# Routed experts: a plain fp32 quarter of the second product, casts on ScalarE alone, one written order

## The chip, the core and the metric

The kernel runs on one core of a Trainium2 chip. The metric is the device time of one execution in microseconds (us). A core has a matrix engine (TensorE, PE in the rows; PEld is its weight load), a vector engine (VectorE, DVE), an activation engine (ScalarE, ACT), GpSimd (POOL), SyncE (SP), which here issues nearly all transfers, and 16 DMA engines. Each engine runs its own instructions in the order in which the program holds them, and waits on semaphores for the others.

## What is computed

The reference chains three parts on 1536 rows (2 batches of 768) of 512 columns, all in fp32. The first is attention with 8 heads, a local window of 96 keys, 8 global keys and a distance bias. The second sends each row with a positive skip score to one of 8 experts; the third runs all 4 experts of a second set on every row and adds them, weighted:

```python
h = np.maximum(xc[mask] @ w1[e], 0.0)            # routed, e of 8: w1 512x1024, w2 1024x512
y[mask] = gate_w[mask, None] * (h @ w2[e])
...
h = np.maximum(x @ w1[e], 0.0)                   # second set, e of 4
out += p[:, e:e + 1] * (h @ w2[e])
```

## The kernel before

**Stages.** Set-up and attention fill the first 131 us of the profiled span: 24 units of half a tile (12 tiles of 128 rows, two groups of heads). Then come the routed experts, to about 262 us, and the second set in 48 steps to the end. This text is mainly on the routed experts.

**One product in three.** Fp32 products are made of `fp32r` matmuls. An operand is split into a high part, a cast to `fp32r`, and a low part, the raw value minus the high part. `mm3` (L108 to L111) then issues three matmuls into the same PSUM bank: high by high (L109), high by low (L110), low by high (L111). A raw weight tile w{i}x is 128x1024 fp32, 512 KB; `split_w` (L91) casts it into one of 12 high tiles (wx0x to wx3x, wh0x to wh7x, used in turn; L97 where ScalarE casts, L101 where GpSimd does), and VectorE subtracts (L68). The low part r{i}x takes the place of w{i}x, one of 20 places.

**One routed expert.** An expert's 128 rows of input are transposed and split into xq (`x_parts`). `layer1` is the first product: 4 weight tiles, 2 banks, 3 matmuls each, so 24 matmuls of 512 columns. `hidden` (L571) takes the ReLU into hs; `h_parts` transposes hs in two halves of four 128x128 blocks and splits them into shh and shl, from the PSUM tile pt; `layer2` (L583 to L587) is the second product: 4 weight tiles, f = 0 to 7, again 24 matmuls, into psy; `rows_of` copies psy to yt (L677) and sends it to memory. The table `SCH_M1` (L106) gives for tile s = 0 to 3 of a product who casts and who subtracts: ScalarE casts s = 0 and 2, GpSimd s = 1 and 3, VectorE does all subtractions.

**What sets the order.** Under `tc.manual_schedule()` an engine's instructions stand as the code calls them. Before, three stretches are under it (the attention loop, the routed experts, the second set), and the set-up ahead of the attention loop is ordered by the scheduler. The loop of the routed experts overlaps neighbours: while PE makes the first product of expert e and then the second of e-1, the other engines split the first weights of e+1, take `hidden` of e, transpose the input of e+1, and split the second weights of e. On ScalarE, for instance, the casts for e+1's first product stand ahead of `hidden` of e. SP fetches weights into the 20 places as the low parts in them have been read for the last time.

**After the routed experts.** The last expert's product is mixed with work for the second set: four tiles of output rows are gathered by GpSimd, sums of the second set's first weights, and their splits.

Of the kernel before, what the change touches and what calls it, by code (L numbers as in the profile page):

```python
# [8 lines left out]
F32 = mybir.dt.float32  # L9
# [35 lines left out]
def attention_moe_moe(ctx: ExitStack, tc: tile.TileContext, qkv, nints_d, wg, w1, w2, dprob, u1, u2, out):  # L45
# [57 lines left out]
                sub_lo(nc.vector if le == "V" else nc.gpsimd, lo[:, a], raw[:, a], hi[:, a])  # L103
        return hi, lo

    SCH_M1 = [[("A", "V")], [("G", "V")], [("A", "V")], [("G", "V")]]  # L106

    def mm3(o, ah, al, bh, bl, start, stop):  # L108
        nc.tensor.matmul(o, ah, bh, start=start, stop=False)  # L109
# [1 line left out]
        nc.tensor.matmul(o, al, bh, start=False, stop=stop)  # L111


    wxx = ExitStack()
    wxp = wxx.enter_context(tc.tile_pool(name="wxp", bufs=1))
    wx = [wxp.tile([P, 1024], F32R, name=f"wx{n}x") for n in range(4)]
# [156 lines left out]
    def load_qk(t):  # L273
        nc.sync.dma_start(qkr[t % 2], qkv[t, :, 0:2])
# [40 lines left out]
    with ExitStack() as c2:  # L315
# [41 lines left out]
        def prep_q(t):  # L357
            qs[t] = qh, ql = xq[t % 2]
            raw = qkr[t % 2][:, 0].rearrange("p (d t) -> p d t", d=NPAIR)
            nc.scalar.activation(out=qh, in_=raw, func=AF.Copy)  # L360
            sub_lo(nc.gpsimd, ql, raw, qh)

        def prep_k(t):
            so = t % 3
            raw = qkr[t % 2][:, 1].rearrange("p (d t) -> p d t", d=NPAIR)
            if t < 2:
                nc.scalar.activation(out=kh[:, so], in_=raw, func=AF.Copy)
            else:
# [12 lines left out]
        def load_gv(t):
            nc.sync.dma_start(gv, qkv[t, 0:GMAX, 2].rearrange("p (h e) -> p h e", h=H))
# [11 lines left out]
        def stage_qk(u):  # L394
            t, g = divmod(u, 2)
            sl, col, ss = slots_of(t)
            nk = len(sl) * P
            qh, ql = qs[t]
            sps[u] = [sbs[(2 * u + n) % 3] for n in range(2)]
            for pp in range(2):  # L400
                pr = 2 * g + pp
                for n, (a, bm) in enumerate(((qh, kh), (qh, kl), (ql, kh))):
                    for h2 in range(2):
                        rows = slice(h2 * HD, (h2 + 1) * HD)
                        nc.tensor.matmul(sps[u][h2][:, pp, 0:nk], a[rows, pr, :], bm[rows, ss, pr, :], start=(n == 0), stop=(n == 2))
# [63 lines left out]
        def run(fs):  # L469
            for f in fs:  # L470
                f()

        NU = 2 * NT
        with tc.manual_schedule():
            load_v(0)
            nc.gpsimd.memset(vv[:, :, :, HD:HV], 1.0)
            prep_q(0)
            prep_k(0)
            save_gk(0)
            load_qk(2)  # L480
            make_bias(slice(512, 640))
            for u in range(-2, NU + 5):
                t, g = divmod(u, 2)
                if u < 2:
                    warm(WARMS[u + 2])
                if u + 2 < NU:
                    stage_qk(u + 2)
                if 0 <= u - 2 < NU:
                    run(norm(u - 2))
                if g == 0:  # L490
                    if 0 <= t - 2 < NT:
                        run(rts[t - 2]["steps"][0])
                    if t + 1 < NT and t >= 0:
                        load_v(t + 1)
                    if t in (0, NI):
                        load_gv(t)
                    if t + 2 < NT and t >= 0:
                        prep_k(t + 2)
                        save_gk(t + 2)
                        prep_q(t + 2)  # L500
                    if t + 4 < NT and t >= 0:
                        load_qk(t + 4)
                    if 0 <= t - 3 < NT:
                        put_row(t - 3)
                else:
                    if 0 <= t - 2 < NT:
                        run(rts[t - 2]["steps"][1])
                    if 0 <= t - 1 < NT and 0 < (t - 1) % NI < NI - 1:
                        over_v(t - 1)
                    if 0 < (t + 1) % NI < NI - 1 and t + 1 < NT:  # L510
                        over_k(t + 1)
                    if 0 <= t < NT:
                        stage_d(t)
                if 0 <= u + 1 < NU:
                    stage_e(u + 1)
                if 0 <= u < NU:
                    stage_t(u, 0)
                    stage_t(u, 1)
                if u + 2 < NU:
                    run(stage_s(u + 2))  # L520
                if u == -2:
                    prep_q(1)
                    prep_k(1)
                    load_qk(3)
                if u == -1:
                    make_bias(slice(0, 512))
                if g == 1 and 0 <= t - 1 < NT:
                    stage_x(t - 1)
                if 0 <= u - 1 < NU:
                    stage_pv(u - 1)  # L530
                if g == 1 and 0 <= t - 1 < NT:
                    rts[t - 1]["lg"] = logits(t - 1, xTs[t - 1], ovt[1])
                if g == 0 and 0 <= t - 2 < NT:
                    rts[t - 2]["rk"] = route_rank(t - 2, rts[t - 2]["lg"])
                if 0 <= u < 4:
                    for e in range(2 * u, 2 * u + 2):
                        nc.sync.dma_start(xs[e * P:(e + 1) * P, :], xr[:, NT - 1, :])
                if u == 4:
                    nc.sync.dma_start(ys[0:1, :], xr[0:1, NT - 1, :])
                if g == 0 and 2 <= t < 2 + 2 * ND:  # L540
                    prefetch((t - 2) * 2, (t - 1) * 2)
                if g == 0 and 4 <= t < 4 + 2 * ND:
                    e_, s_ = divmod(t - 4, ND)
                    split_w(wts[t - 4], (wx if e_ else his)[s_], [("A", "V")])
                if u == 6:
                    shares()
                if u == NU - 2:
                    exs.append(qkr[0][:, 0])
                    for t_ in range(NT - NSEL, NT):
                        sels[t_] = a3.tile([P, P], F32, name="sel", tag="sc", bufs=12)  # L550
                if u == NU + 1:
                    pt0, frs = first_rows(ovt[0])
                    frs[0]()
                if u == NU + 2:
                    frs[1]()
            frs[2]()
            split_psum(*xq[0], pt0)
    lpx.close()


# [11 lines left out]
        return hs  # L572

    def h_parts(hs, pool, pst, hp=None, ns=range(2)):
        hh, hl = hp if hp else (pool.tile([P, NF, P], F32R, name=f"sh{m}") for m in "hl")
        pts = {n: transp4(pst, hs[:, n * 512:(n + 1) * 512], tag="pst") for n in ns}
        for n in ns:
            split_psum(hh[:, 4 * n:4 * n + 4, :], hl[:, 4 * n:4 * n + 4, :], pts[n])
        return hh, hl

    def layer2(py, hp, w2s, fs):
        for f in fs:
            w = w2s[f // 2]  # L583
            c = slice((f % 2) * 512, (f % 2) * 512 + 512)
            mm3(py, hp[0][:, f, :], hp[1][:, f, :], w[0][:, c], w[1][:, c], f == 0, f == NF - 1)

    bufs2 = [wts[4:10], wts[10:16]]  # L587

# [14 lines left out]
    with ExitStack() as c2:  # L603
# [3 lines left out]
        psx = c2.enter_context(tc.tile_pool(name="psx", bufs=1, space=PSUM))  # L607
        pst = c2.enter_context(tc.tile_pool(name="pst", bufs=2, space=PSUM))
        psy = c2.enter_context(tc.tile_pool(name="psy", bufs=1, space=PSUM))
        c2.enter_context(tc.manual_schedule())  # L610
        for n in range(2 * ND, NWT):
            raw1[order1[n]] = wts[n]
        nwt[0] = NWT
# [20 lines left out]

        def split1(e, half, part=range(ND)):
            nwh[0] += ND if part[0] == 0 else 0
            return [split_w(raw1[e, half * ND + s], whs[(nwh[0] - ND + s) % 12], SCH_M1[s]) for s in part]

        slf = mp.tile([P, NT], F32, name="slf", bufs=1)
        hps = w2s = None  # L640
# [122 lines left out]
    with ExitStack() as c2:  # L763
        xp = c2.enter_context(tc.tile_pool(name="xp", bufs=1))
        yp = c2.enter_context(tc.tile_pool(name="yp", bufs=3))
        ps = c2.enter_context(tc.tile_pool(name="ps", bufs=1, space=PSUM))
        c2.enter_context(tc.manual_schedule())
        xh = xp.tile([P, 7, 2, T // 2], F32R, name="xh")
        xl = xp.tile([P, 7, 2, T // 2], F32R, name="xl")
        t4 = [xp.tile([P, 2, P], F32, name=f"t4{n}x") for n in range(2)]  # L770
# [179 lines left out]
            pend = (q, c, (hh, hl))  # L950


    ok = nc.values_load(badi[0:1, 0:1], min_val=0, max_val=1)
    with tc.If(ok < 1):
        general(nc, tc, dict(qkv=qkv, ngv=ngv, nlv=nlv, colf=colf, rowf=rowf, xr=xr, ident=ident, transp4=transp4, pas=pas, pr=pr, wgt=wgt,
# [203 lines left out]
```

## Time and profile before

| what | number |
|---|---|
| time, median of 3 runs (772.71, 772.85, 778.5) | 772.85 us |
| the profiled execution: its time, its span | 777.55 us, 775.6 us |
| mean granted TensorE clock over the span, share of full | 0.975 |
| PE busy over the span | 740.3 us (95%) |
| VectorE, ScalarE, GpSimd busy | 550.7 (71%), 294.7 (38%), 294.5 (38%) us |
| chain that ended last, by engine | PE 62%, the others 2% or less each |

The profile is one execution; its span is the time from the first to the last instruction, so 1.95 us of its time lie outside the span. A window row cuts the span and gives for a stretch each engine's busy time and its count of instructions, the granted TensorE clock, the mean busy share of the 16 DMA engines, and what they moved. A waits row says which engine and line waited, for which tile of which engine, for how many us in total, how often, and the longest. A timeline row is one instruction: its start, its duration, engine, line, operation, out<-in, and in brackets how long its engine had been idle before and who ended that. PE's durations overlap, since matmuls are pipelined: what one costs is the distance to the next one's start.

### The profile page before, as it was taken

How to read it: one execution, taken by the hardware profiler on the slowest of the kernel's cores; microseconds unless marked ns; L12 is line 12 of the kernel's file. 1: busy time of each engine (PE TensorE's matmuls, PEld its weight loads, DVE VectorE, ACT ScalarE, POOL GpSimd, SP SyncE). 2: the span in 40 equal slices, each digit the busy share in tenths (PEclk: the TensorE clock that was granted, in tenths of full speed). 3: DMA queues.
4: the chain of work that ended last, by engine and by line, in shares of the span. 5: the costliest groups of instructions: out<-in, count | busy, mean ns of one | idle time of the engine just before them, and what ended most of it. 6: DMA issues, size and time to landing. Idle time of an engine off the chain costs nothing.

```text
span 775.6 us, 12245 instructions
## 1 busy us (share of the span) xinstructions
PE 740.3 (95%) x4810; PEld 665.5 (86%) x4810; DVE 550.7 (71%) x1032; ACT 294.7 (38%) x461; POOL 294.5 (38%) x272
## 2 busy tenths in 40 slices
PE   6999996998889989999999999999999999999996
PEld 6999995876667878999999999999999999999995
DVE  7686875699996979666666666666766666666665
ACT  3876871365353555432232222322322222223111
POOL 5564633244356741474152341441423415314000
PEclk8997998999899999999999999999999999999999
DMA  5866712799663120110010010000100110001003
GB/s 145 283 211 199 239 32 78 282 411 347 238 219 108 55 69 1 53 57 28 28 55 28 28 55 28 28 28 28 55 28 27 49 34 28 28 28 55 1 28 140
DMA packets 36020, 74.90 MB, mean 97 GB/s; under 512 B 15960, under 2 KB 16216, under 8 KB 35954
## 3 DMA queue, kind: packets, MB, share of 16 engines
q1 hardware_dynamic: 34034, 69.39, 26.2%
q0 software_dynamic: 1920, 4.64, 1.9%
q8 instruction: 40, 0.66, 0.3%
q14 instruction: 26, 0.21, 0.1%
HBM read 65.19 MB, written 10.49 MB: 98 GB/s over the span
## 4 chain that ended last, share of the span: by engine, by line
PE 62%; DVE 2%; issue 2%; POOL 2%; DMA 1%; ACT 0%; POOLq 0%; DVEq 0%
PE pf L110 5%; PE pf L109 5%; PE pf L111 5%; PE pg L109 4%; PE pg L110 4%; PE pg L111 4%; PE pa3x L109 3%; PE pa3x L111 3%; PE pa3x L110 3%; PE pa1x L110 3%; PE pa0x L109 3%; PE pa1x L111 3%; PE pa0x L110 3%; PE pa0x L111 3%; PE pa1x L109 3%; PE pa2x L110 3%
## 5 line engine op out<-in xcount | busy, mean ns | idle before, releaser
L908 DVE TENSOR_TENSOR cc<-pg,sf 128x768 f32<-128x768 f32 x48 | 45.9, 957 | 56.8 <-PE pg L111 55.4
L890 ACT ACTIVATE sf<-pf 128x768 f32<-128x768 f32 x48 | 38.9, 811 | 107.3 <-PE pf L111 107.3
L932 ACT ACTIVATE hh0x<-cc 128x1024 fp32r<-128x1024 f32 x24 | 25.5, 1061 | 120.7 <-DVE cc L917 120.7
L932 ACT ACTIVATE hh1x<-cc 128x1024 fp32r<-128x1024 f32 x23 | 24.4, 1060 | 106.4 <-DVE cc L917 106.4
L917 DVE TENSOR_TENSOR cc<-cc,uv 128x768 f32<-128x768 f32 x47 | 52.7, 1121 | 1.6
L933 DVE SCALAR_TENSOR_TENSOR hl0x<-cc,hh0x 128x1024 fp32r<-128x1024 f32 x24 | 29.5, 1231 | 24.8 <-ACT hh0x L932 24.8
L933 DVE SCALAR_TENSOR_TENSOR hl1x<-cc,hh1x 128x1024 fp32r<-128x1024 f32 x23 | 28.5, 1240 | 25.0 <-ACT hh1x L932 25.0
L592 POOL TENSOR_TENSOR w6x<-w4x 128x256 f32<-128x256 f32 x8 | 9.9, 1244 | 94.0 <-DMA w4x<-in_u_dram 94.0
L592 POOL TENSOR_TENSOR w12x<-w10x 128x256 f32<-128x256 f32 x8 | 9.9, 1241 | 92.1 <-DMA w10x<-in_u_dram 92.1
L891 DVE TENSOR_TENSOR uv<-pf,sf 128x256 f32<-128x256 f32 x48 | 20.4, 424 | 34.1 <-ACT sf L890 34.1
L110 PE MATMUL pf<-xl,r8x 128*128 128x256 f32 x144 | 40.8, 284 | 2.7 <-DVE xl L68 2.7
L851 DVE SCALAR_TENSOR_TENSOR xr<-pa2x,pr,xr 128x512 f32<-128x512 f32 x44 | 33.0, 750 | 13.3 <-PE pa2x L111 13.2
L109 PE MATMUL pf<-xh,r8x 128*128 128x256 f32 x144 | 40.6, 282 | 0.0
L111 PE MATMUL pf<-xh,r6x 128*128 128x256 f32 x144 | 40.5, 281 | 0.0
L110 PE MATMUL pf<-xl,r14x 128*128 128x256 f32 x144 | 40.5, 281 | 0.0
L109 PE MATMUL pf<-xh,r14x 128*128 128x256 f32 x144 | 40.5, 281 | 0.0
L111 PE MATMUL pf<-xh,r12x 128*128 128x256 f32 x144 | 40.5, 281 | 0.0
L851 DVE SCALAR_TENSOR_TENSOR xr<-pa1x,pr,xr 128x512 f32<-128x512 f32 (+1 forms) x46 | 34.0, 738 | 2.3 <-PE pa1x L111 2.3
L851 DVE SCALAR_TENSOR_TENSOR xr<-pa0x,pr,xr 128x512 f32<-128x512 f32 (+1 forms) x46 | 33.9, 736 | 1.3 <-PE pa0x L111 1.3
L851 DVE SCALAR_TENSOR_TENSOR xr<-pa3x,pr,xr 128x512 f32<-128x512 f32 x45 | 33.5, 744 | 0.6 <-PE pa3x L111 0.6
L68 POOL TENSOR_TENSOR r11x<-w11x,r15x 128x1024 fp32r<-128x1024 f32 x7 | 16.9, 2421 | 35.9 <-ACT r15x L97 35.9
L68 POOL TENSOR_TENSOR r5x<-w5x,r9x 128x1024 fp32r<-128x1024 f32 x7 | 16.8, 2394 | 35.8 <-ACT r9x L97 35.8
(1220 smaller groups left out, 2778.6 us busy)
## 6 DMA issues: line engine op xcount, KB each, us to landing
w4x<-in_u_dram SPq DMA_DIRECT2D x8, 512.0 KB, 3.3
w5x<-in_u_dram SPq DMA_DIRECT2D x8, 512.0 KB, 3.3
w10x<-in_u_dram SPq DMA_DIRECT2D x8, 512.0 KB, 3.4
w11x<-in_u_dram SPq DMA_DIRECT2D x8, 512.0 KB, 3.4
qk1x<-in_qkv_dram SPq DMA_DIRECT2D x6, 512.0 KB, 4.0
vv<-in_qkv_dram SPq DMA_DIRECT2D x12, 256.0 KB, 4.6
out_dram<-xr SPq DMA_DIRECT2D x11, 256.0 KB, 2.0
qk0x<-in_qkv_dram SPq DMA_DIRECT2D x5, 512.0 KB, 4.2
```

Of the source, the lines that this page charges most:

```text
L68: eng.tensor_tensor(out=lo, in0=src, in1=hi.bitcast(F32), op=ALU.subtract)
L109: nc.tensor.matmul(o, ah, bh, start=start, stop=False)
L110: nc.tensor.matmul(o, ah, bl, start=False, stop=False)
L111: nc.tensor.matmul(o, al, bh, start=False, stop=stop)
L592: eng.tensor_tensor(out=sm[:, 0], in0=a21, in1=a22, op=ALU.add)
L851: nc.vector.scalar_tensor_tensor(out=acc[:, tt, cs], in0=ac[:, cs], scalar=pr[:, tt, e:e + 1], in1=acc[:, tt, cs], op0=ALU.mult, op1=ALU.add)
L890: nc.scalar.activation(out=sf, in_=pf[:, 0:3], func=AF.Copy)
L891: tt(out=uv, in0=pf[:, 3], in1=sf[:, 0], op=ALU.add)
L908: tt(out=cc[:, 0:3], in0=pg, in1=sf, op=ALU.add)
L917: tt(out=cc[:, 1:4], in0=cc[:, 1:4], in1=uv.unsqueeze(1).to_broadcast([P, 3, 256]), op=ALU.add)
L932: nc.scalar.activation(out=hh, in_=cc, func=AF.Relu)
L933: nc.vector.scalar_tensor_tensor(out=hl, in0=cc, scalar=0.0, in1=hh.bitcast(F32), op0=ALU.max, op1=ALU.subtract)
```

## The change

There are three parts. One: the three stretches of written order become one, from before the first pools to the end, so that the set-up is written order too. Two: `SCH_M1` has one entry, so ScalarE makes every cast of the routed experts and GpSimd none. Three: tile s = 3 of each second product is no longer split. `layer2` multiplies it, for f = 6 and 7, in one plain fp32 matmul each, with an unsplit fp32 copy of the last two blocks of h (`shf`), which ScalarE makes; shh and shl have six blocks instead of eight. The diff, without the attention loop, which only moves four columns to the left:

```diff
-    SCH_M1 = [[("A", "V")], [("G", "V")], [("A", "V")], [("G", "V")]]
+    SCH_M1 = [("A", "V")]
...
+    ordered = ExitStack()
+    ordered.enter_context(tc.manual_schedule())
     wxx = ExitStack()
...
-        with tc.manual_schedule():
...
     def h_parts(hs, pool, pst, hp=None, ns=range(2)):
-        hh, hl = hp if hp else (pool.tile([P, NF, P], F32R, name=f"sh{m}") for m in "hl")
+        hh, hl, hf = hp if hp else [pool.tile([P, NF - 2, P], F32R, name=f"sh{m}") for m in "hl"] + [pool.tile([P, 2, P], F32, name="shf")]
         pts = {n: transp4(pst, hs[:, n * 512:(n + 1) * 512], tag="pst") for n in ns}
         for n in ns:
-            split_psum(hh[:, 4 * n:4 * n + 4, :], hl[:, 4 * n:4 * n + 4, :], pts[n])
-        return hh, hl
+            k = slice(4 * n, 4 * n + 4 - 2 * n)
+            split_psum(hh[:, k, :], hl[:, k, :], pts[n][:, 0:4 - 2 * n])
+            if n:
+                nc.scalar.activation(out=hf, in_=pts[n][:, 2:4], func=AF.Copy)
+        return hh, hl, hf
...
-            mm3(py, hp[0][:, f, :], hp[1][:, f, :], w[0][:, c], w[1][:, c], f == 0, f == NF - 1)
+            if w[1] is None:
+                nc.tensor.matmul(py, hp[2][:, f - NF + 2, :], w[0][:, c], start=f == 0, stop=f == NF - 1)
+            else:
+                mm3(py, hp[0][:, f, :], hp[1][:, f, :], w[0][:, c], w[1][:, c], f == 0, f == NF - 1)
...
-        c2.enter_context(tc.manual_schedule())
...
-            return [split_w(raw1[e, half * ND + s], whs[(nwh[0] - ND + s) % 12], SCH_M1[s]) for s in part]
+            return [(raw1[e, half * ND + s][0], None) if half and s == ND - 1 else split_w(raw1[e, half * ND + s], whs[(nwh[0] - ND + s) % 12], SCH_M1)
+                    for s in part]
...
-        c2.enter_context(tc.manual_schedule())
...
+    ordered.close()
```

The order moves on VectorE, ScalarE, GpSimd and PE; SP's is the same row for row. Three places follow. The first is VectorE where the routed experts begin: slot is the last of the routing, xq01x the low part of expert 0's input, r8x to r12x low parts of weights. Before:

```order
L192 CAST slot<-sl 128x1
L68 TENSOR_TENSOR r8x<-w8x,wh0x 128x1024
L68 TENSOR_TENSOR xq01x<-ov0x,xq00x 128x512
L68 TENSOR_TENSOR r9x<-w9x,wh1x 128x1024
L68 TENSOR_TENSOR xq11x<-pt,xq10x 128x512
L68 TENSOR_TENSOR r10x<-w10x,wh2x 128x1024
L68 TENSOR_TENSOR r11x<-w11x,wh3x 128x1024
L68 TENSOR_TENSOR shl<-pt,shh 128x512 x2
L68 TENSOR_TENSOR r12x<-w12x,wh4x 128x1024
```

The same place with the change:

```order
L194 CAST slot<-sl 128x1
L68 TENSOR_TENSOR xq01x<-ov0x,xq00x 128x512
L68 TENSOR_TENSOR r8x<-w8x,wh0x 128x1024
L68 TENSOR_TENSOR r9x<-w9x,wh1x 128x1024
L68 TENSOR_TENSOR xq11x<-pt,xq10x 128x512
L68 TENSOR_TENSOR r10x<-w10x,wh2x 128x1024
L68 TENSOR_TENSOR shl<-pt,shh 128x512
L68 TENSOR_TENSOR shl<-pt,shh 128x256
L68 TENSOR_TENSOR r12x<-w12x,wh4x 128x1024
```

The subtraction xq01x moves ahead of r8x; r11x, the low part of the tile that is no longer split, is gone, and the second shl is half as wide.

The second place is ScalarE in one turn of the experts' loop: casts of the next expert's first weights, `hidden` (hs), the next input, casts of second weights, the split of h, and yt. Before:

```order
L97 ACTIVATE wh2x<-w2x 128x1024
L571 ACTIVATE hs<-pa0x 128x512
L571 ACTIVATE hs<-pa1x 128x512
L283 ACTIVATE xq10x<-pt 128x512
L97 ACTIVATE wh4x<-w4x 128x1024
L97 ACTIVATE wh6x<-w6x 128x1024
L283 ACTIVATE shh<-pt 128x512 x2
L677 ACTIVATE yt<-psy 128x512
```

With the change:

```order
L97 ACTIVATE wh2x<-w2x 128x1024
L97 ACTIVATE wh3x<-w3x 128x1024
L572 ACTIVATE hs<-pa0x 128x512
L572 ACTIVATE hs<-pa1x 128x512
L285 ACTIVATE xq10x<-pt 128x512
L97 ACTIVATE wh4x<-w4x 128x1024
L97 ACTIVATE wh5x<-w5x 128x1024
L97 ACTIVATE wh6x<-w6x 128x1024
L285 ACTIVATE shh<-pt 128x512
L285 ACTIVATE shh<-pt 128x256
L582 ACTIVATE shf<-pt 128x256
L684 ACTIVATE yt<-psy 128x512
```

Two more casts stand ahead of hs (wh3x, and wh1x ahead of the rows shown), one more (wh5x) ahead of the split of h, and the second half of that split is cut into a cast and a copy.

The third place is VectorE in the set-up: kl is the low part of tile 0's keys, xr here the distances, tri and base constants, bias the table that the scores need. Before:

```order
L303 SCALAR_TENSOR_TENSOR bad<-nval,okt 128x1
L68 TENSOR_TENSOR kl<-qk0x,kh 128x512
L305 TENSOR_SCALAR xr<-xr,nval 128x640
L304 TENSOR_SCALAR xr<-xr,nval 128x640
L308 TENSOR_SCALAR tri<-colf,rowf 128x128
L306 TENSOR_TENSOR xr<-xr 128x640
L309 TENSOR_SCALAR base<-colf 128x8
L307 SCALAR_TENSOR_TENSOR xr<-xr,nval 128x640
L328 TENSOR_SCALAR bias<-xr 128x128 x8
```

With the change:

```order
L305 SCALAR_TENSOR_TENSOR bad<-nval,okt 128x1
L306 TENSOR_SCALAR xr<-xr,nval 128x640
L307 TENSOR_SCALAR xr<-xr,nval 128x640
L308 TENSOR_TENSOR xr<-xr 128x640
L309 SCALAR_TENSOR_TENSOR xr<-xr,nval 128x640
L310 TENSOR_SCALAR tri<-colf,rowf 128x128
L311 TENSOR_SCALAR base<-colf 128x8
L68 TENSOR_TENSOR kl<-qk0x,kh 128x512
L330 TENSOR_SCALAR bias<-xr 128x128 x8
```

kl moves from the head of this list to just ahead of bias.

## Rows read from the trace of the kernel before

**Rows 1.** Windows: stretch; length, busy us (count) of PE, PEld, DVE, ACT, POOL; clock, DMA share, GB/s.

```profile
0.00:20.00 20.00, 13.74 (x83) 12.56 (x84) 15.08 (x58) 7.75 (x18) 10.22 (x24) 0.83 0.55 149
20.00:56.00 36.00, 36.00 (x359) 34.29 (x357) 26.27 (x142) 30.00 (x67) 23.63 (x33) 1.00 0.78 257
56.00:68.00 12.00, 12.00 (x77) 11.78 (x76) 5.77 (x33) 6.44 (x15) 4.22 (x7) 0.57 0.53 171
131.00:240.00 109.00, 95.05 (x425) 76.00 (x426) 98.58 (x91) 48.87 (x70) 45.11 (x31) 0.94 0.77 282
```

**Rows 2.** Waits of PE, 131 to 240 us: who waited for whom: total us, times, longest.

```profile
PE pa0x L111 <- DVE xq01x L68: 4.0, 1, 4.0
PE pt L279 <- DVE xq11x L68: 3.8, 1, 3.8
PE py L111 <- DVE shl L68: 3.2, 1, 3.2
PE psy L111 <- DVE shl L68: 3.0, 3, 2.1
```

**Rows 3.** Timeline of DVE, around 131 and 222 us: start, duration, instruction.

```profile
130.49 4.57 DVE L68 TENSOR_TENSOR r8x<-w8x,wh0x 128x1024 fp32r<-128x1024 f32 x1 [1.89 <-ACT wh0x L97]
134.98 0.68 DVE L68 TENSOR_TENSOR xq01x<-ov0x,xq00x 128x512 fp32r<-128x512 f32 x1
...
221.82 1.21 DVE L68 TENSOR_TENSOR r13x<-w13x,wx1x 128x1024 fp32r<-128x1024 f32 x1
222.95 2.06 DVE L68 TENSOR_TENSOR r14x<-w14x,wx2x 128x1024 fp32r<-128x1024 f32 x1
```

**Rows 4.** Timeline of POOL: the first of four casts in a row, and one at 222 us.

```profile
129.90 1.07 POOL L101 TENSOR_SCALAR wh1x<-w9x 128x1024 fp32r<-128x1024 f32 x1
...
222.56 1.37 POOL L101 TENSOR_SCALAR wh3x<-w19x 128x1024 fp32r<-128x1024 f32 x1 [1.74 <-PE pa1x L111]
```

**Rows 5.** Timeline of ACT: a cast, hs behind it, and yt of two experts in turn.

```profile
170.76 1.05 ACT L97 ACTIVATE wx2x<-w10x 128x1024 fp32r<-128x1024 f32 x1
174.34 0.60 ACT L571 ACTIVATE hs<-pa2x 128x512 f32<-128x512 f32 x1 [2.53 <-PE pa2x L111]
...
216.95 0.60 ACT L677 ACTIVATE yt<-psy 128x512 f32<-128x512 f32 x1 [2.13 <-PE psy L111]
...
229.38 0.60 ACT L677 ACTIVATE yt<-psy 128x512 f32<-128x512 f32 x1 [2.13 <-PE psy L111]
```

**Rows 6.** Timeline of PE: two matmuls after the first long wait, and two in full flow.

```profile
136.31 0.63 PE L109 MATMUL pa1x<-r16x,xq00x 128*128 128x512 f32 x1
136.73 0.63 PE L110 MATMUL pa1x<-r0x,xq00x 128*128 128x512 f32 x1
...
223.22 0.39 PE L111 MATMUL psy<-wh4x,shl 128*128 128x512 f32 x1
223.45 0.39 PE L109 MATMUL psy<-wh4x,shh 128*128 128x512 f32 x1
```

**Rows 7.** Plain fp32 matmuls of line 237: count, ns least/median/most, first and last start.

```profile
L237 PE MATMUL pa1x<-selt,ylast x8: 274/275/276, 257.8 to 258.6; 128*128 128x128 f32 x8
```

**Rows 8.** Timeline of PE: eight plain fp32 records of 65 columns in attention.

```profile
21.62 1.00 PE L449 MATMUL ov0x<-vv,ptb0x 128*128 128x65 f32 x8
```

**Rows 9.** Timeline of DVE in the set-up.

```profile
6.18 1.21 DVE L68 TENSOR_TENSOR kl<-qk0x,kh 128x512 fp32r<-128x512 f32 x1 [1.05 <-ACT kh L367]
7.31 0.41 DVE L305 TENSOR_SCALAR xr<-xr,nval 128x640 bf16<-128x640 bf16 x1
```

**Rows 10.** Timeline of PE: the first matmul after its longest wait in the set-up.

```profile
13.84 0.47 PE L405 MATMUL pa2x<-kh,xq00x 64*128 64x128 f32 x1 [4.46 <-DVE mn L416]
```

**Rows 11.** Windows, columns as in rows 1: ten microseconds of the routed experts.

```profile
170.00:180.00 10.00, 7.90 (x37) 6.12 (x36) 9.90 (x13) 5.38 (x7) 3.63 (x3) 1.00 0.85 311
```

**Rows 12.** DMA issues, 120 to 262 us: tile, queue, count, KB each, median us to landing.

```profile
w11x<-in_w_dram SPq DMA_DIRECT2D x2, 512.0 KB, 7.8
```

**Rows 13.** Timeline of SP: the issue of one weight tile.

```profile
156.06 0.33 SPq L81 DMA_DIRECT2D w11x<-in_w_dram  x1
```

More of the change, by code (lines that the diff above doesn't have):

```diff
@@ L473, in attention_moe_moe @@
         NU = 2 * NT
-        with tc.manual_schedule():
[L475 to L557, printed above, removed]
@@ new lines, in attention_moe_moe @@
+        load_v(0)
+        nc.gpsimd.memset(vv[:, :, :, HD:HV], 1.0)
+        prep_q(0)
+        prep_k(0)
+        save_gk(0)
+        load_qk(2)
+        make_bias(slice(512, 640))
+        for u in range(-2, NU + 5):
+            t, g = divmod(u, 2)
+            if u < 2:
+                warm(WARMS[u + 2])
+            if u + 2 < NU:
+                stage_qk(u + 2)
+            if 0 <= u - 2 < NU:
+                run(norm(u - 2))
+            if g == 0:
+                if 0 <= t - 2 < NT:
+                    run(rts[t - 2]["steps"][0])
+                if t + 1 < NT and t >= 0:
+                    load_v(t + 1)
+                if t in (0, NI):
+                    load_gv(t)
+                if t + 2 < NT and t >= 0:
+                    prep_k(t + 2)
+                    save_gk(t + 2)
+                    prep_q(t + 2)
+                if t + 4 < NT and t >= 0:
+                    load_qk(t + 4)
+                if 0 <= t - 3 < NT:
+                    put_row(t - 3)
+            else:
+                if 0 <= t - 2 < NT:
+                    run(rts[t - 2]["steps"][1])
+                if 0 <= t - 1 < NT and 0 < (t - 1) % NI < NI - 1:
+                    over_v(t - 1)
+                if 0 < (t + 1) % NI < NI - 1 and t + 1 < NT:
+                    over_k(t + 1)
+                if 0 <= t < NT:
+                    stage_d(t)
+            if 0 <= u + 1 < NU:
+                stage_e(u + 1)
+            if 0 <= u < NU:
+                stage_t(u, 0)
+                stage_t(u, 1)
+            if u + 2 < NU:
+                run(stage_s(u + 2))
+            if u == -2:
+                prep_q(1)
+                prep_k(1)
+                load_qk(3)
+            if u == -1:
+                make_bias(slice(0, 512))
+            if g == 1 and 0 <= t - 1 < NT:
+                stage_x(t - 1)
+            if 0 <= u - 1 < NU:
+                stage_pv(u - 1)
+            if g == 1 and 0 <= t - 1 < NT:
+                rts[t - 1]["lg"] = logits(t - 1, xTs[t - 1], ovt[1])
+            if g == 0 and 0 <= t - 2 < NT:
+                rts[t - 2]["rk"] = route_rank(t - 2, rts[t - 2]["lg"])
+            if 0 <= u < 4:
+                for e in range(2 * u, 2 * u + 2):
+                    nc.sync.dma_start(xs[e * P:(e + 1) * P, :], xr[:, NT - 1, :])
+            if u == 4:
+                nc.sync.dma_start(ys[0:1, :], xr[0:1, NT - 1, :])
+            if g == 0 and 2 <= t < 2 + 2 * ND:
+                prefetch((t - 2) * 2, (t - 1) * 2)
+            if g == 0 and 4 <= t < 4 + 2 * ND:
+                e_, s_ = divmod(t - 4, ND)
+                split_w(wts[t - 4], (wx if e_ else his)[s_], [("A", "V")])
+            if u == 6:
+                shares()
+            if u == NU - 2:
+                exs.append(qkr[0][:, 0])
+                for t_ in range(NT - NSEL, NT):
+                    sels[t_] = a3.tile([P, P], F32, name="sel", tag="sc", bufs=12)
+            if u == NU + 1:
+                pt0, frs = first_rows(ovt[0])
+                frs[0]()
+            if u == NU + 2:
+                frs[1]()
@@ L558, in attention_moe_moe @@
+        frs[2]()
+        split_psum(*xq[0], pt0)
     lpx.close()
@@ L584, in layer2 @@
             c = slice((f % 2) * 512, (f % 2) * 512 + 512)
-            mm3(py, hp[0][:, f, :], hp[1][:, f, :], w[0][:, c], w[1][:, c], f == 0, f == NF - 1)
+            if w[1] is None:
+                nc.tensor.matmul(py, hp[2][:, f - NF + 2, :], w[0][:, c], start=f == 0, stop=f == NF - 1)
+            else:
+                mm3(py, hp[0][:, f, :], hp[1][:, f, :], w[0][:, c], w[1][:, c], f == 0, f == NF - 1)
     bufs2 = [wts[4:10], wts[10:16]]
```

## The prediction

> **What bounds the kernel now.** I read the windows first, to find the stretch where PE isn't full. From 131 to 240 us, the routed experts, PE is busy 95.05 of 109 us and its clock averages 0.94 of full, while VectorE is busy 98.58 us, more than PE; ScalarE and GpSimd are below half [rows 1]. The waits of PE in this stretch name one engine: four entries, all on VectorE, 4.0 + 3.8 + 3.2 + 3.0 = 14.0 us [rows 2]. So VectorE bounds this stretch, and PE bounds most of the rest. The timeline of VectorE shows why. A subtraction of a whole weight tile costs 1.13 us from start to start (221.82 to 222.95), but the next takes 2.06 [rows 3]. A GpSimd cast runs from 222.56 to 223.93, over most of it [rows 4]. At the head it is worse: r8x takes 4.57 us while four GpSimd casts run back to back from 129.90, and xq01x, for which PE waits, starts only behind it at 134.98 [rows 3, 4]. So GpSimd's casts and VectorE's subtractions hold each other up.
>
> VectorE's turn for one expert is 8 subtractions at 1.13, 0.6 for xq and 1.2 for the two shl, 10.8 us; with about three of them 0.85 longer (2.06 for 1.21), 13.4. PE's turn, where it is undisturbed, is 229.38 - 216.95 = 12.43 us, from yt to yt [rows 5]. VectorE is the longer by a microsecond and falls back until PE waits.
>
> **GpSimd takes no casts, VectorE one subtraction less.** VectorE's turn becomes 7 x 1.13 + 0.6 + 0.95 = 9.5 us with nothing against it, 3 us below PE's. The three entries behind the first, 10.0 us, should go. The first, 4.0, goes by two changes at once: xq01x stands ahead of r8x, and the four casts are gone. Together -14.0. Bounds: -14.0, and -7 if half comes back as other waits.
>
> **The clock.** After the first long wait a matmul costs 136.73 - 136.31 = 0.42 us, in full flow 0.23 [rows 6]: that is 1.2 GHz against 2.4 GHz. The stretch's mean clock of 0.94 means 0.06 x 109 = 6.5 us lost at most [rows 1]; some of the low clock falls on time when PE waits, which is counted already. I take -5.5, with 0 and -6.5 as ends. The Trainium skill ("TensorE: Matmul & The Clock Gate", Part 1) says that the array's clock is throttled by default, that activity releases it and idling brings the throttle back; by that all of the 6.5 would go with the waits, and the sum would be 1 us lower. The trace agrees as far as it shows low clock behind long waits; but 56 to 68 us [rows 1] is at 0.57 with PE busy throughout, so waits are not all of it.
>
> **Plain fp32 matmuls.** Each of 8 experts exchanges 6 fp32r matmuls of 512 columns (6 x 0.23 = 1.38 us) for 2 plain ones. The trace has none of that width. The nearest row has 128 columns: 8 records for 4 matmuls, starting over 0.8 us, about 0.11 each, 0.22 a matmul [rows 7]. Four times as wide is 0.88, two are 1.76, so +0.38 per expert and +3.0 in all. The upper end is attention's 65-column rows: 8 records in 1.00, two to a matmul, 0.25 per 65 columns, 1.97 per 512 [rows 8], which gives +2.56 per expert, +20.5. The lower end is a record at the pitch of an fp32r matmul, two records per matmul: 4 x 0.23 = 0.92 for 1.38, -3.7. I take the first, since 128 columns lie nearest to 512 and cost less per column than 65. The Trainium skill (same page, "Weight-path perf modes") says that the fast weight load is off for fp32 data, which speaks against the change; if the load set the pace, it would come out at the upper end. No row here shows a 512-column load of that kind, but even at 65 columns the whole record took 0.125 us, and a record of 512 columns should take about 0.44, so that a load would hide behind it.
>
> **ScalarE.** It takes two more casts of about 1 us ahead of hs (its casts start 0.95 apart and last 1.05 [rows 5]), one more ahead of the split of h, and an extra copy shf, under 0.6. Its turn is then 7 casts x 0.95 + hs 1.0 + xq 0.5 + split 1.1 + yt 0.5 = 9.8 us, against PE's 12.8: it has room on the whole. The tight place is hs. Before, ScalarE sat idle 2.53 us until PE finished the first product [rows 5]; two casts leave 0.4 to 0.6. What is late next, if hs comes late, is the transposes of h. PE reaches these only after the first half of the other second product, 12 x 0.23 = 2.8 us. So nothing is lost unless ScalarE falls over 3 us behind. I add +0.5 for the first turns, where the buffers are not yet full; ends 0 and +6.
>
> **The order.** In the set-up VectorE makes kl at 6.18 and the distances from 7.31 [rows 9]. With kl behind them they can start at about 5.1, 2.2 us earlier; kl costs its 1.13 before bias, so bias and the first scores come 1.1 earlier. PE then waits for VectorE's mn, 4.46 us until 13.84 [rows 10], so that moves attention as a whole: -1.1. kl itself is later, and PE's first scores with it, in time that PE now idles. Ends: 0, and -4.5 if the shorter wait also keeps the clock up (0.83 over the first 20 us, so 0.17 x 20 = 3.4 more [rows 1]). At the head of the routed experts the order's effect is in the 4.0 above. SP's order is unchanged, so transfers are issued when their place comes free, earlier if anything, since tile s = 3 is read by PE at the same place.
>
> **The sum.** -14.0 - 5.5 + 3.0 + 0.5 - 1.1 = -17.1 us. The profiled execution of 777.55 (span 775.6 and 1.95 outside) would be 760.45. That execution lies 4.7 above the median of 772.85, and has a stretch that may explain it: from 56 to 68 us PE does 77 matmuls at a clock of 0.57 with no idle time, where 359 in 36 us, so 120 in 12, is the pace before [rows 1]: 12 x (1 - 77/120) = 4.3 us. Two of three runs are near 772.8. The change doesn't touch this stretch, so I take the sum from the median: 755.8. After the routed experts PE is the bound, and its chain starts from the last yt, so the gain carries to the end.
>
> **Rivals.** A measurement of this kernel tells about 1% (7.7 us) from no change, so faster is below 765.1 and slower above 780.6.
> - A, as summed: 755.8, by its own terms 752 to 761.
> - B, the wait moves to ScalarE: hs comes later than PE can absorb, by about one cast in each of six full turns, 6 x 1.05 = 6.3, so 762. For it: the 0.4 to 0.6 us left before hs. Against: the 2.8 us behind it.
> - C, the low-clock stretch of attention falls on the median run too: +4.3, 760. One or two of the four executions seen had it.
> - D, the transfers become the bound. An expert needs 8 weight tiles of 512 KB [rows 12] and rows in and out of 256 KB each, 4608 KB or 4.72 MB. At the 311 GB/s of 170 to 180 us [rows 11] that takes 15.2 us, 2.4 over PE's 12.8, in six turns +14.4, so 770. Against: this rate was reached with the transfers waiting for places, and a weight tile issued at 156.06 [rows 13] lands 7.8 us later [rows 12], at 163.9, where ScalarE makes the cast ahead of its own at 170.76 [rows 5].
> - E, slower: ScalarE in strict order is held by a late weight tile, s = 1 or 3 of the next expert, ahead of hs; before, GpSimd took that wait. For over 780.6 it must lose 24.8 us, 4.1 per turn in six turns, beyond the 3.3 it can absorb. The tile would have to be there 7.4 us later than it is needed; by the rows above it is there about 8 us before.
> - F, the plain matmul costs what attention's rows cost: +20.5 in place of +3.0, so 773.3, no change.
>
> **How the numbers follow.** A 0.57, B 0.15, C 0.12, D 0.06, E 0.06, F 0.04. The time is A's, 755.8. The range reaches from 751, where the set-up gains its 4.5 and the clock its 6.5 (755.8 - 3.4 - 1.0 = 751.4), up to 767, over B and C and part of D; about 0.85. Faster: A, B and C, 0.84; same: D and F, 0.10; slower: E, 0.06.
>
> **What would show it.** In the profile after: no entry of PE on VectorE over 1 us from 131 to 240 us; every whole-tile subtraction near 1.2 us; no GpSimd casts; PE's two plain matmuls in about 1.8 us; yt to yt about 12.8; the stage near 93 us for 109. If PE waits on ScalarE for hs or shh, it is B or E; if on a weight tile, D. If PE's waits vanish and the time doesn't fall, my account of what bounds the stretch is wrong.

## The result, and the profile after

The changed kernel takes 755.11 us (median of four runs, 754.9 to 756.36), the kernel before 773.2 beside it: a ratio of 0.9744, 95% interval 0.9698 to 0.979. Timed again among the experiments it took 755.15 us, ratio 0.9749 (0.9717 to 0.9781). The forecast was 755.8.

The profiled execution took 756.36 us, its span is 754.6, 21.0 us shorter than the span before. To see where, take three stretches: up to the first matmul of the routed experts (`pa0x<-r16x`), from there to the first matmul `pf<-xh,r8x` of the second set, and the rest. The rows below are PE's at these two places, first before, then with the change: a timeline row, and a row of one group of instructions with its first and last start.

```profile
131.00 0.50 PE L109 MATMUL pa0x<-r16x,xq00x 128*128 128x512 f32 x1 [0.86 <-ACT xq00x L283]
L109 PE MATMUL pf<-xh,r8x x144: 277/281/383, 262.9 to 724.4; 128*128 128x256 f32 x144
```

```profile
127.40 0.50 PE L109 MATMUL pa0x<-r16x,xq00x 128*128 128x512 f32 x1 [0.74 <-ACT xq00x L285]
L109 PE MATMUL pf<-xh,r8x x144: 276/281/387, 242.1 to 703.0; 128*128 128x256 f32 x144
```

| stretch | before | after | difference |
|---|---|---|---|
| set-up and attention | 131.0 | 127.4 | -3.6 |
| routed experts, to the second set's first pf | 131.9 | 114.7 | -17.2 |
| the rest of the span | 512.7 | 512.5 | -0.2 |

The first row's 3.6 us are not all of the change: the execution before has the low clock from 56 to 68 us [rows 1], about 4.3 us by the prediction's working, and that of after hasn't (the second row below).

In the windows of the kernel after, PE fills the routed stretch and its clock is full; rows 1 have 95.05 of 109 us at 0.94 for about the same work (425 matmul records there, 407 here). GpSimd went from 45 us to under 6, ScalarE from 48.87 to 67.36, VectorE from 98.58 to 68.99.

```profile
0.00:20.00 20.00, 16.77 (x104) 15.01 (x105) 15.60 (x64) 9.61 (x23) 10.80 (x27) 0.83 0.65 176
56.00:68.00 12.00, 12.00 (x123) 11.39 (x120) 8.90 (x47) 9.76 (x23) 7.31 (x9) 1.00 0.78 256
131.00:221.00 90.00, 89.78 (x407) 68.45 (x406) 68.99 (x81) 67.36 (x99) 5.68 (x4) 1.00 0.89 336
```

Of PE's waits in this stretch, 14.0 us on VectorE [rows 2], one of 0.2 is left, beside the 0.7 on ScalarE at the head:

```profile
PE pa0x L109 <- ACT xq00x L285: 0.7, 1, 0.7
PE py L111 <- DVE shl L68: 0.2, 1, 0.2
```

VectorE's timeline shows both causes of rows 3 gone. xq01x comes first, r8x takes 1.23 for 4.57, and two subtractions in a row in mid-stage take 1.22 each, 1.14 from start to start:

```profile
127.38 0.69 DVE L68 TENSOR_TENSOR xq01x<-ov0x,xq00x 128x512 fp32r<-128x512 f32 x1 [3.12 <-ACT xq00x L285]
128.32 1.23 DVE L68 TENSOR_TENSOR r8x<-w8x,wh0x 128x1024 fp32r<-128x1024 f32 x1 [0.26 <-ACT wh0x L97]
...
154.36 1.22 DVE L68 TENSOR_TENSOR r1x<-w1x,wh1x 128x1024 fp32r<-128x1024 f32 x1
155.50 1.22 DVE L68 TENSOR_TENSOR r2x<-w2x,wh2x 128x1024 fp32r<-128x1024 f32 x1
```

In the set-up VectorE goes straight on to the distances, kl stands behind them, and PE's wait of 4.46 us until 13.84 [rows 10] is 0.34 until 11.64 (two rows of VectorE, one of PE). Ahead of that PE now waits 1.67 us for kl, until 8.94:

```profile
4.93 0.38 DVE L306 TENSOR_SCALAR xr<-xr,nval 128x640 bf16<-128x640 bf16 x1
...
8.20 0.69 DVE L68 TENSOR_TENSOR kl<-qk0x,kh 128x512 fp32r<-128x512 f32 x1
```

```profile
11.64 0.47 PE L407 MATMUL pa2x<-kh,xq00x 64*128 64x128 f32 x1 [0.34 <-DVE mn L418]
```

### The profile page after: what moved, and what is told of

The parts are those of the page before. It is cut to its first block, busy times and chain, and to the rows that moved or that the text cites. A ratio compares the mean times of both kernels' runs of the same rounds, so it can differ in the third digit from the quotient of the medians.

```text
span 754.6 us, 12189 instructions
## 1 busy us (share of the span) xinstructions
PE 736.4 (98%) x4794; PEld 657.3 (87%) x4794; DVE 522.1 (69%) x1024; ACT 312.7 (41%) x489; POOL 252.8 (33%) x244
## 4 chain that ended last, share of the span: by engine, by line
PE 87%; DVE 5%; DMA 3%; issue 2%; ACT 2%; POOL 0%; POOLq 0%; ACTq 0%; DVEq 0%
PE pf L110 6%; PE pf L109 6%; PE pf L111 6%; PE pg L109 4%; PE pg L110 4%; PE pg L111 4%; PE pa0x L111 3%; PE pa0x L109 3%; PE pa1x L110 3%; PE pa0x L110 3%; PE pa1x L109 3%; PE pa3x L109 3%; PE pa3x L111 3%; PE pa1x L111 3%; PE pa3x L110 3%; PE pa2x L111 3%
## 5 line engine op out<-in xcount | busy, mean ns | idle before, releaser
L110 PEld LDWEIGHTS pf<-xl,r8x 128*128 128x128 f32 x144 | 27.0, 188 | 3.4 <-issue 2.5
```

What stands on the lines that cost most here:

```text
L110: nc.tensor.matmul(o, ah, bl, start=False, stop=False)
```

## The experiments

My theory: VectorE's subtractions, held up by GpSimd's passes over SBUF tiles, bound the routed stage; taking GpSimd's passes away ends that, and PE is then the bound. The main rivals are that VectorE's count of subtractions is what matters (so that the plain quarter is needed), that the order of VectorE's work is, or that waiting for GpSimd to make a cast is, not its being busy. The table gives every run; "stage" is the routed stretch as above, read in that run's profile. T is the theory and R with a number a rival, as the expectations name them. The runs were timed in three groups, in which the kernel before took 772.28 us (order alone and the three pairs), 773.71 (the change, half plain, idle passes, expert 6) and 772.74 (casts alone and the last two), so between groups the ratios say more than the medians.

| kernel | median us | ratio to before, 95% | stage us |
|---|---|---|---|
| before | 772 to 774 | 1 | 131.9 |
| order alone | 764.16 | 0.9894 (0.9864 to 0.9924) | 123.5 |
| casts on ScalarE alone | 755.74 | 0.9782 (0.974 to 0.9823) | 113.2 |
| order + casts | 753.59 | 0.9744 (0.9714 to 0.9775) | 114.8 |
| order + plain quarter | 761.69 | 0.9873 (0.9834 to 0.9912) | 120.4 |
| casts + plain quarter | 755.99 | 0.9792 (0.976 to 0.9824) | 115.0 |
| all three (the change), second timing | 755.15 | 0.9749 (0.9717 to 0.9781) | 114.7 |
| all three, half plain | 756.89 | 0.9778 (0.9744 to 0.9811) | 115.7 |
| order + casts + idle GpSimd passes | 768.37 | 0.9924 (0.9895 to 0.9953) | 127.5 |
| order + casts, plain in expert 6 only | 753.17 | 0.9743 (0.9699 to 0.9787) | 111.6 |
| order + casts, sums on VectorE | 751.48 | 0.97 (0.9663 to 0.9737) | 111.3 |
| the last, 14 more warming matmuls | 750.88 | 0.9707 (0.9669 to 0.9744) | 111.3 |

### Each part alone, and in pairs

**The order alone.** The two lines that open one order, and the three old ones gone:

```diff
+    ordered = ExitStack()
+    ordered.enter_context(tc.manual_schedule())
```

> Part one alone: one written order, with the splits and the second product as before. Theory T (VectorE's subtractions, held up by GpSimd's casts, bound the routed stage; the order gives its own gain in the set-up and at the stage's head): 2.2 us from the set-up, 2 to 4 at the head, the other three entries of PE's waits (10 us) stay: 767 to 769 us. Rival R1 (VectorE is behind anyway, what the head gives is lost later): only the set-up's 2.2 stay, 771.

Measured 764.2, 3 us under T's range. PE's waits in its stage:

```profile
PE py L111 <- DVE shl L68: 3.2, 1, 3.2
PE pt L281 <- DVE xq11x L68: 2.7, 1, 2.7
PE psy L111 <- DVE shl L68: 2.4, 2, 2.1
```

The three entries stay, as T said, but at 8.3 us, not 10.0, since VectorE starts its row of subtractions earlier; with the 4.0 at the head gone that is -5.7. The stage's mean clock is 0.97 for 0.95 (lost 0.03 x 123.5 = 3.7 us for 0.05 x 131.9 = 6.6), 2.9 more. Together that is about the 8.4 by which the stage shrank; T had left the clock out. R1 is refuted, by the time and by the waits.

**Order and casts, no plain quarter.**

```diff
-    SCH_M1 = [[("A", "V")], [("G", "V")], [("A", "V")], [("G", "V")]]
+    SCH_M1 = [[("A", "V")]] * 4
```

> Parts one and two: written order and every cast on ScalarE, but all tiles split, no plain fp32. Theory T: VectorE's turn for an expert is 8 x 1.13 + 0.6 + 1.2 = 10.8 us with GpSimd out of the way, under PE's 12.43, so PE's waits on VectorE are gone without part three, and the 3.0 us that the plain matmuls cost come back: 752 us. Rival R2 (the subtraction and the cast that part three drops are needed, ScalarE has 8 casts a turn): hs or shl late in each turn, 757 us or more.

Measured 753.6, and the psy and pt waits on VectorE are gone with all eight tiles split. One wait on VectorE is left, where expert 6's h meets the second product (`py`):

```profile
PE py L111 <- DVE shl L68: 1.9, 1, 1.9
```

So the casts alone do it: R2 is refuted for all turns but this one. Its cause stands in the same profile. GpSimd is back for the second set's sums, and four subtractions take 1.49 to 1.76 us instead of 1.22 (first VectorE, then GpSimd):

```profile
204.45 1.75 DVE L68 TENSOR_TENSOR r17x<-w17x,wh1x 128x1024 fp32r<-128x1024 f32 x1
206.13 1.76 DVE L68 TENSOR_TENSOR r18x<-w18x,wh2x 128x1024 fp32r<-128x1024 f32 x1
```

```profile
203.41 1.71 POOL L595 TENSOR_TENSOR w6x<-w4x 128x256 f32<-128x256 f32 x1
205.09 1.72 POOL L596 TENSOR_TENSOR w6x<-w6x,w4x 128x256 f32<-128x256 f32 x1
```

**Order and the plain quarter, GpSimd keeps its casts.** `SCH_M1` as before, `h_parts`, `layer2` and `split1` as in the change.

> Parts one and three: written order and the plain fp32 quarter, but GpSimd keeps its casts (s = 1 and 3 of w1, s = 1 of w2). Theory T: VectorE's turn is 7 x 1.13 + 0.95 + 0.6 and about three subtractions 0.85 longer, 12.0 us, under PE's 12.8, so most waits go here too: 757 to 760 us. Rival R3 (the hold-ups by GpSimd alone make the waits): entries of 2 to 4 us on VectorE stay, 765 us or more.

Measured 761.7, between the two, nearer to T. Waits for shl, 5.6 us with the order alone, fell to 0.3, but the one for xq11x grew to 4.0:

```profile
PE pt L281 <- DVE xq11x L68: 4.0, 1, 4.0
PE py L111 <- DVE shl L68: 0.3, 1, 0.3
```

It falls in the turn of expert 4, where one more transposition wants the same PSUM tile and so waits for xq11x earlier, behind two subtractions of 2.07 and 2.05 us. Some of it is part three's own: just ahead of the row of subtractions VectorE stood idle 1.89 us for a cast, which ScalarE began late, since shf, the copy for the plain matmuls, had waited 6.57 us for VectorE's shl (ScalarE, then VectorE):

```profile
177.18 0.38 ACT L583 ACTIVATE shf<-pt 128x256 f32<-128x256 f32 x1 [6.57 <-DVE shl L68]
179.03 1.22 DVE L68 TENSOR_TENSOR r16x<-w16x,wh4x 128x1024 fp32r<-128x1024 f32 x1 [1.89 <-ACT wh4x L97]
```

One subtraction fewer relieves VectorE's average, but not a place at which two held-up ones stand in a row.

**Casts and plain quarter, three stretches of order as before.**

> Parts two and three without part one: the set-up as the scheduler orders it, r8x ahead of xq01x. Theory T: the set-up's 2.2 us are lost and about 1.2 at the head, where PE waits for xq01x behind one undisturbed subtraction: 758.5 us. Rival R4 (the order does nothing that counts, since attention is bound elsewhere): 755 us.

Measured 756.0, 0.8 above the change's 755.15 by the medians and 3.3 by the ratios (0.9792, 0.9749), with overlapping intervals: this doesn't decide between T and R4. The set-up's wait is as it was before, which settles whose it is:

```profile
13.69 0.47 PE L405 MATMUL pa2x<-kh,xq00x 64*128 64x128 f32 x1 [4.46 <-DVE mn L416]
```

The stage, 115.0, is only 0.3 above the change's. Up to the routed experts the kernel takes 128.08 us for 127.4: of the 2 us of the set-up 0.7 arrive in this profile, since low clock at the end of attention differs from run to run (last section).

**Casts alone**, on the kernel before, with the diff of the second run only.

> Part two alone: every cast on ScalarE, all tiles split, three stretches of order as before. Theory T (part two alone undoes the hold-ups; part one adds the set-up's 2 us and about 0.3 in the stage): 755 to 757 us, stage 115 us for 131.9. Rival R10 (order and casts each give about 8 us in the stage, and add up): 761 to 763 us.

Measured 755.7. R10 is refuted: order and casts don't add up. In the stage the order is worth 8.4 us while GpSimd makes casts and nothing once it doesn't (113.2 against 114.8; the latter has a low clock, 0.90 from 208 to 225 us, behind its one wait, while casts alone, with a wait of 1.7 us at the same place, have 1.00 there). Part two alone gives 17 of the 18 us.

### Is it GpSimd's being busy?

Order and casts, and behind each odd tile's cast a pass that nobody waits for:

```diff
+                if s % 2:
+                    nc.gpsimd.tensor_scalar(out=idle, in0=got[-1][0].bitcast(F32), scalar1=1.0, scalar2=1.0, op0=ALU.mult, op1=ALU.mult)
```

> Parts one and two with all tiles split (753.6 us), and on GpSimd, behind each cast of s = 1 and 3, one pass over the high tile just made into a tile that nobody reads: as many passes as GpSimd had casts, of the same size, none of which anything waits for but the reuse of the high tile 12 tiles later. Theory T (GpSimd's passes hold up VectorE's subtractions): VectorE's turn is 10.8 + 3 to 4 x 0.85 = 13.4 to 14.2 us, over PE's 12.43, subtractions of about 2.06 us are back, PE's waits too: 761 to 766 us. Rival R5 (what counted was waiting for GpSimd to cast, not its being busy): 753 to 755 us.

Measured 768.4: 14.8 us more than without the passes by the medians, 13.9 by the ratios, and 2.4 beyond T's upper end; R5 is refuted. Nothing but GpSimd's passes and their one tile differs, no engine waits for a pass in the profile, and the 2.06 us subtractions are back. GpSimd's pass, 1.05 where it has the way free, takes 1.9 (VectorE first):

```profile
169.71 2.06 DVE L68 TENSOR_TENSOR r9x<-w9x,wx1x 128x1024 fp32r<-128x1024 f32 x1
171.69 2.06 DVE L68 TENSOR_TENSOR r10x<-w10x,wx2x 128x1024 fp32r<-128x1024 f32 x1
```

```profile
168.79 1.91 POOL L642 TENSOR_SCALAR idle<-wh1x 128x1024 f32<-128x1024 f32 x1 [2.40 <-ACT wh1x L97]
170.78 1.90 POOL L642 TENSOR_SCALAR idle<-wh3x 128x1024 f32<-128x1024 f32 x1
```

The Trainium skill ("SBUF — State Buffer", "SBUF: two separate sides") states that VectorE and GpSimd take a shared pair of ports by an exclusive lock: an operation of VectorE with two SBUF inputs and one of GpSimd that reads SBUF shut each other out for a whole instruction. The trace agrees: the pass of 168.79 ends at 170.70 and the subtraction beside it at 171.77, the pass of 170.78 at 172.68 and the next subtraction at 173.75. Each subtraction thus ends 1.07 us after the pass, about the 1.14 that an undisturbed one takes from start to start.

### What the plain matmuls cost

**The change, timed again.**

> The changed kernel again, beside the others on one chip. Theory T: part three gives nothing of its own once parts one and two are there, and costs 3 us of matmul time, less what is left of waits on VectorE without it (1.9 us in the run with all tiles split): 754 to 756 us, 1 to 2 above that kernel. Rival R2 (part three is needed): at least 2 us below it.

Measured 755.15, 1.6 above the kernel without part three by the medians, 0.4 by the ratios, with overlapping intervals (0.9717 to 0.9781, 0.9714 to 0.9775). R2 is refuted; that the part costs time is shown by the traces more than by these times.

**Half of each second product plain**, s = 2 and 3. Besides the line shown, shf becomes a copy of the whole second PSUM tile of h:

```diff
-            return [(raw1[e, half * ND + s][0], None) if half and s == ND - 1 else split_w(raw1[e, half * ND + s], whs[(nwh[0] - ND + s) % 12], SCH_M1)
+            return [(raw1[e, half * ND + s][0], None) if half and s >= ND - 2 else split_w(raw1[e, half * ND + s], whs[(nwh[0] - ND + s) % 12], SCH_M1)
```

> The changed kernel with half of each second product in plain fp32 (s = 2 and 3) in place of a quarter: 6 fp32r matmuls fewer and 2 plain ones more per expert. Theory T (PE bounds the stage now; two plain matmuls cost 1.73 us for 1.38): 8 x 0.35 = 2.8 us more than the changed kernel, 758 us. Rival R6 (VectorE or ScalarE still bounds; one more tile without a split gives time back): 755 us or less.

Measured 756.9, +1.7 for T's +2.8. R6 is refuted. The size is seen in PE's period, from one expert's transposition of hs to the next. First all tiles split (the kernel with the sums on VectorE), then the change, then half plain:

```profile
143.21 1.04 PE L281 MATMUL pt<-ident,hs 128*128 128x128 f32 x8
155.64 1.03 PE L281 MATMUL pt<-ident,hs 128*128 128x128 f32 x8
```

```profile
143.56 1.14 PE L281 MATMUL pt<-ident,hs 128*128 128x128 f32 x8
156.57 1.14 PE L281 MATMUL pt<-ident,hs 128*128 128x128 f32 x8
169.43 1.03 PE L281 MATMUL pt<-ident,hs 128*128 128x128 f32 x8
182.20 1.03 PE L281 MATMUL pt<-ident,hs 128*128 128x128 f32 x8
```

```profile
143.46 1.03 PE L281 MATMUL pt<-ident,hs 128*128 128x128 f32 x8
156.54 1.04 PE L281 MATMUL pt<-ident,hs 128*128 128x128 f32 x8
```

That is 12.43, then 13.01, 12.86 and 12.77, then 13.08: 0.34 for the first quarter once it has settled, 0.31 for the second. The change's first two turns are 0.24 and 0.09 longer, since ScalarE is late there. With half plain that is gone, and so the second quarter seems cheaper in the total. The two engines have less to do there, but the traces show a nearer cause: in the change each of the eight copies shf waits for VectorE's shl, which reads the same PSUM tile, 15.6 us in all; with half plain shf has its tile to itself, no such wait is left, and ScalarE starts hs in the same turn at 152.89 us for 155.92.

### GpSimd's last hold-up, and a faster kernel

**Plain fp32 in expert 6 only.** As order and casts, but `split1`'s condition has `and e == E1 - 2`.

> Parts one and two, with plain fp32 only in expert 6's second product, where PE still waits 1.9 us for shl. Theory T: the wait goes, 0.35 us of matmul time comes: 752 us, 1.5 below the kernel with all tiles split. Rival R7 (the wait is followed by another): no difference, 753.6.

The py wait is gone and the stage is 111.6 for 114.8 (1.6 of that may be the low clock, since casts alone have 113.2 with the wait), but the median, 753.17, hardly moved: attention took 127.59 us in this profile and 125.33 in the other, with the same instructions. By the time, R7 isn't refuted; by the stage, T is right.

**The sums on VectorE**, in time in which it was idle:

```diff
-        sums_moe2(bufs2[0], nc.gpsimd)
+        sums_moe2(bufs2[0], nc.vector)
```

> Parts one and two with all tiles split, and the four sums for the second set's first weights, which GpSimd makes from 202.7 to 208.5 us in that kernel while four subtractions on VectorE take 1.75 us instead of 1.22, are made by VectorE behind its last subtraction of the stage, where it is idle 3.44 us. Theory T (these sums are GpSimd's last hold-up of VectorE, and the cause of PE's last wait of 1.9 us): the wait goes, and with it some low clock: stage 111 to 112 us for 114.8, time 750.5 to 751.5. Rival R8 (the wait comes of VectorE's own number of subtractions): 753.6.

Measured 751.5, ratio 0.97, stage 111.3, as T has it and not R8. All subtractions are there, the count on VectorE grew by four, and the wait is gone. The sums take 0.42 us each on VectorE. In its stage PE waits for nothing but the head:

```profile
PE pa0x L109 <- ACT xq00x L285: 0.7, 1, 0.7
```

This is 3.7 us under the change's 755.15 by median; the two ratios' intervals (0.9663 to 0.9737, 0.9717 to 0.9781) overlap a little.

**More warming matmuls ahead of the first scores.**

```diff
-WARMS = (2, 6, 6, 6)
+WARMS = (16, 6, 6, 6)
```

> As the run with the sums on VectorE, with 14 more of the matmuls that only keep PE busy, ahead of its first scores, where it now waits 1.7 to 2.5 us for kl. Theory T2 (the low clock from about 9 to 18 us comes of this wait): clock near 1.00 over the first 20 us for 0.83, PE's work there ends up to 3 us earlier: 748 to 750 us. Rival R9 (VectorE's chain sets the pace of the first units whatever PE's clock, or the clock falls anyway): within 1 us of that run.

Measured 750.9, ratio 0.9707, as R9 has it. The wait for kl is 1.2 us for 1.9, but the clock fell as before:

```profile
8.00:20.00 12.00, 10.19 (x74) 9.01 (x75) 10.62 (x48) 6.14 (x18) 5.50 (x8) 0.72 0.63 179
20.00:52.00 32.00, 32.00 (x321) 30.55 (x319) 23.58 (x126) 26.01 (x58) 20.95 (x30) 1.00 0.83 264
52.00:68.00 16.00, 16.00 (x114) 15.75 (x115) 8.64 (x48) 9.60 (x22) 8.21 (x9) 0.68 0.47 145
```

The wait isn't wholly filled, so T2's cause isn't excluded.

## Why the prediction was right, step by step

- **What bounds the stage** was right: VectorE, held up by GpSimd. The idle passes, which only occupy GpSimd, brought 12.7 of the stage's 17 us back. One reading was loose: the cast of rows 4 covers 0.98 of the 2.06 us (222.95 to 223.93), not most of them, and the subtraction ends 1.08 us behind it, as with the idle passes.
- **Casts off GpSimd, waits -14.0**: of the four entries 0.2 us is left, so -13.8. But I gave two causes for the waits in one breath, GpSimd's hold-ups and the number of subtractions, and the account leaned on VectorE's turn of 9.5 us with seven. With eight, 10.8, it fits as well: the first cause was enough.
- **The clock, -5.5**: the stretch went from 0.94 to 1.00, so nearly the whole 6.5 came back. The Trainium skill ("TensorE: Matmul & The Clock Gate", Part 1: idling brings the throttle back) would have had it so, and this stretch agrees. My discount for low clock during waits was too large by about 1 us.
- **Plain matmuls, +3.0**: 0.34 per expert, 2.7 in all. A plain fp32 record of 512 columns starts every 0.43 us, four to an expert:

```profile
L590 PE MATMUL psy<-w19x,shf x4: 592/592/592, 158.9 to 160.2; 128*128 128x512 f32 x4
```

  Three distances in 1.3 us. So the price scaled from the row with 128 columns was right, and F, the price of attention's 65-column rows, is refuted. The loads of these records (190 ns) lie under the records.
- **ScalarE, +0.5**: the size was right, 0.24 + 0.09 in two turns, the account of the room wasn't. I had 0.4 to 0.6 us left ahead of hs. In the trace there is none: ScalarE does hs straight behind its casts, with no idle time, long after PE is done with pa0x (one row of PE, then ScalarE from shf on):

```profile
152.28 0.39 PE L111 MATMUL pa0x<-wh7x,xq01x 128*128 128x512 f32 x1
```

```profile
151.37 0.39 ACT L582 ACTIVATE shf<-pt 128x256 f32<-128x256 f32 x1 [1.84 <-DVE shl L68]
151.65 0.59 ACT L684 ACTIVATE yt<-psy 128x512 f32<-128x512 f32 x1
152.13 1.06 ACT L97 ACTIVATE wh0x<-w0x 128x1024 fp32r<-128x1024 f32 x1
...
154.97 1.05 ACT L97 ACTIVATE wh3x<-w3x 128x1024 fp32r<-128x1024 f32 x1
155.92 0.59 ACT L572 ACTIVATE hs<-pa0x 128x512 f32<-128x512 f32 x1
```

  The casts begin only behind yt, and yt behind shf, which waits 1.84 us for VectorE's shl. I had counted ScalarE's work, not this row of waits in its order. hs starts 3.2 us after pa0x is done (152.28 + 0.39), and only PE's half product of 2.8 us, the cover that I named, hid nearly all of it. Most of the room went to part three's copy, not to the casts: with all tiles split (the kernel with the sums on VectorE) hs starts 1.95 us ahead of its transposition (153.69, 155.64), here 0.65 (155.92, 156.57). Why two readers of one PSUM tile stand behind each other, no run shows. B's mechanism is thus in the profile, and it stopped just short of costing more; that 0.5 came out right is partly luck.
- **The order, -1.1 in the set-up**: -2.2 (13.84 to 11.64). Half of what was missing is kl, 1.13 by rows 9, which costs 0.60 from start to start at its new place; the rest comes in pieces of about 0.2 (the distances start at 4.93 for my 5.1 and take less, bias takes 2.16 for 2.39). What lengthened kl before I didn't test, but GpSimd's subtraction ran beside its first half, up to 6.84, and none beside it at 8.20 in the trace after, so it may be the same hold-up:

```profile
5.55 1.29 POOL L68 TENSOR_TENSOR xq01x<-qk0x,xq00x 128x512 fp32r<-128x512 f32 x1 [1.83 <-ACT xq00x L360]
```

  The clock of the first 20 us stayed at 0.83, so the further 3.4 of that term's lower end didn't come; two other profiles with the set-up of before (casts alone, casts and plain quarter) have 0.78 and 0.76 there, so it isn't the same from run to run. Apart from the set-up and the 4.0 at the head, which the casts' removal would have given too, the order is worth nothing here.
- **The sum.** -13.8 - 6.5 + 2.7 + 0.3 = -17.3 for the stage, which shrank by 17.2; I had -16.0. Against the medians, -18.1 was measured, -17.1 forecast. The profiled execution before had the low clock of 56 to 68 us, which that of after didn't (0.57 [rows 1], 1.00 above), and taking the sum from the median was right. C didn't happen to the median. Part of the closeness is luck: 17.2 and the set-up's 2.2 make 19.4, so about 1 us of the set-up's gain didn't arrive. Had it arrived, the forecast would have been 2 us off and not 1.
- **D and E**: the transfers kept pace at 336 GB/s in the mean. In the routed stretch neither PE nor ScalarE nor VectorE has a wait that names the transfer of a weight tile.

## What to carry to other kernels

When VectorE is the bound, look at what GpSimd does while VectorE's instructions run long: two durations of one form, 1.21 and 2.06 us here, are a better lead than the busy shares, and moving the other engine's work was worth more here than shortening VectorE's own (18.7 us for order and casts, 10.6 for order and plain quarter). Test such a cause with a pass that nobody waits for. Before costing an extra piece on an engine, follow what stands ahead of it in that engine's order and what each of these waits for, and whether the new piece itself has to wait, as shf did; the sum of its work says little about when it comes to the tight instruction.

## What the runs showed of the hardware that I had not expected

The clock of attention isn't the same from run to run. The stretch at low clock with PE fully busy (56 to 68 us before, at 0.57) is in one other of the thirteen profiles, that with the warming matmuls (52 to 68 us, 0.68), and both are executions some 5 us above their kernel's median. What starts it I can't say. Kernels with the same instructions up to the routed experts reached these at 124.37 to 127.59 us in their profiles, with low clock somewhere between 112 and 128 us, behind short matmuls and waits at attention's end. How long it lasts differs: by the mean clocks of windows of 4 us it costs, as an estimate, 3.4 us with the order alone (0.92, 0.50 and 0.72 from 112 to 124 us) and 6.8 with the change. In the profile after, for instance:

```profile
112.00:116.00 4.00, 3.74 (x21) 3.64 (x21) 1.82 (x10) 0.00 (x0) 0.00 (x0) 0.57 0.29 77
...
120.00:124.00 4.00, 4.00 (x21) 3.94 (x22) 1.57 (x12) 0.00 (x0) 0.25 (x2) 0.50 0.07 24
```

So a gain of 2 us ahead of that, as in the set-up, is seen in the trace and not clearly in the time: without the order the kernels are 0.8 us (casts and plain quarter) and 2.2 us (casts alone) slower by the medians, 3.3 and 2.9 by the ratios, each with overlapping intervals.
